# A 128-long, overlapping last chunk of keys, and a new order for the first batch and the last store, in a packed attention with a gated FFN

## The chip, the cores and the metric

The kernel runs on 1 core of one Trainium2 chip. The metric is the device time of one execution in microseconds (us). Before the change the median of 3 runs was 719.26 us, the lowest 718.98 and the highest 720.36.

## The reference

There are 8 batches, 8 heads, 576 tokens, a head width of 64, and 32 packed queries p per batch and head. Two attentions follow each other, and their output goes through a feed-forward network with a sigmoid gate:

```
P   = softmax(p k^T / 8) v            # 32 x 64 for each batch and head
x   = softmax(q P^T / 8) P            # 576 x 64 for each batch and head
h   = x @ w_in                        # x as 4608 x 512, w_in 512 x 2048
out = (h * sigmoid(1.702 h)) @ w_out  # w_out 2048 x 512
```

All of it is float32.

## The kernel before, in words

**Tiling.** The batches are worked one after the other, the first attention of batch b+1 inside the FFN of batch b. Heads go in pairs: of a pair the even head (eo = 0) lies on partitions 0 to 63 and the odd one on 64 to 127, so a 64-row product of one parity and one of the other use the two halves of TensorE's rows. The FFN is never done on x itself: `m_chunk` (L399) multiplies the small P with w_in, giving M (for each parity a tile of 128 rows: 4 heads of 32 packed queries), and `h_mm` (L561) multiplies M with the second attention's weights `a`. Large products are kept accurate by splitting each float32 operand into an upper and a lower part (`ghi`/`glo`, `mhi`/`mlo`, `ahi`/`alo`, and both halves of `wo`) and adding three products.

**FFN of a batch.** For each of 16 blocks f of 128 hidden columns: six matmuls per half of the tokens (288), tanh on ACT (L569), the gate on DVE (L551), the upper part on ACT or DVE (L116, L118), the lower part on POOL or DVE (L548), and three matmuls 128x512 per block of 128 tokens (L621) into one of four PSUM banks `acc`. 576 tokens are four blocks of 128 and a rest of 64. The rests of two batches (a pair) are gathered in the tiles `over` and make one more product of 128 tokens, `over_mm`, into bank acc0 (`acc_over` in the profile). `over_take` copies that bank to SBUF in two halves of 256 columns, and `over_store` stores each half: 2 batches x 64 rows x 256 columns. For the last pair this is the end of the program: the two copies, on ACT (L116) and DVE (L118), and the two stores (L660).

**First attention of a batch.** Scores of p with the keys (L247), in two halves of 288 keys; a maximum (L272 in batch 0), exp (`exp1`, L318; L311 in batch 0); then the weights are transposed. `turn1_mm` (L337) transposes four chunks of 128 keys per parity, `turn1_last_mm` (L348) the last 64 keys of both, and `turn1_copy` and `turn1_last_copy` copy them from PSUM to the tile `aT`. `pack` (L370) multiplies them with v: for each parity five chunks of keys, and in each chunk four products of 32 packed queries by 64 columns, which lie side by side on TensorE's columns. Each float32 product takes two passes, so a batch has 2 x 5 x 4 x 2 = 80 rows in the trace. Chunks 0 to 3 have 128 keys ("128*32" in the profile: 128 rows, 32 columns of the array), chunk 4 has 64 ("64*32"). `pack_end` (L383) divides by the sums on ACT, `pack_turn_mm` (L389) transposes P. v is loaded as two parts: `v` (512 keys) and `v_last` (64 keys, 64 partitions x 2 KB).

**Second attention.** `scores2_mm` (L451), DVE's `scores2_turn` (L462), `max2` (L482), POOL's `sub2` (L486), exp on ACT (L490), `sum2` (L495 to L497), `norm2` on POOL, and `turn2` (L507) back to key-major, whose result `xt` is split into `ahi` and `alo` for `h_mm`. For batch 0 the lower part is made on TensorE (`a_lower_mm`, L522 and L523).

**Weights.** w_in and w_out arrive as 8-byte words and are decoded: `load_w` (SP's queue), `begin_w` (ACT, L205), `join_w` (DVE, L217); `upper_w` and `lower_w` (L229) split w_out. Entries 0 to 3 of the list are the four row blocks of w_in's first 512 columns, loaded in two halves, 4 to 7 the first four blocks of w_out, and so on. `warm` (L124) issues matmuls of the identity that nobody uses.

**Order.** Nothing is scheduled by a program: the tuple `order` (L668 and on) lists every step, and each engine gets its instructions in that order; the steps take the engine as an argument (`dve`, `act`, `pool`), ACT being what most take without one. All loads and stores are issued by SP.

Of the kernel before, what the change touches and what calls it, by code (L numbers as in the profile page):

```python
# [21 lines left out]
def kernel(  # L22
# [111 lines left out]
    def load(what, b, part):  # L134
# [124 lines left out]
    def scores1_first(eo, half):  # L259

        if half == 0:
            new1(0, eo)
        if eo == 1:
            bank = ps_acc.tile([P, FC], F32, tag=f"acc{half}", name=f"ps1_0_{eo}_{half}")
        else:
            bank = bank_b(f"ps1_0_{eo}_{half}")
        for j in range(NP):
            mm1(0, eo, half, bank, j)
        st["bank", eo, half] = bank
# [60 lines left out]

    def turn1_mm(b, eo):
# [13 lines left out]
    def turn1_last_mm(b):  # L345
        st["bank", "t", b] = bank = bank_b(f"pstl_{b}")
        for e in range(2):
            nc.tensor.transpose(  # L348
                bank[:KLAST, e * P : (e + 1) * P], st["x", 1, b, e][:, (KC - 1) * P :], ident
            )  # L350

    def turn1_last_copy(b, engine=nc.scalar):
        move(
            engine,
            st["aT", b][:KLAST, KC - 1, :, :],
            st["bank", "t", b][:KLAST, : 2 * P].rearrange("p (e n) -> p e n", n=P),
        )

    def pack(b, eo=None, banks=(bank_b,)):
# [4 lines left out]
        for e in range(2) if eo is None else (eo,):  # L364
            bank = st["bank", "P", b][e if len(st["bank", "P", b]) > 1 else 0]
            for c in range(KC):
                kk = P if c < KC - 1 else KLAST
                for j in range(NP):
# [3 lines left out]
                        aT[:kk, c, e, 32 * j : 32 * j + 32],  # L372
                        vt[:kk, c, e0 : e0 + D],
# [277 lines left out]

    def over_take(pair, k, engine=nc.scalar):
        if k == 0 or pair == B // 2 - 1:
            taken["over"] = o_tile(f"o_over_{pair}_{k}")
        taken["over", pair, k] = o = taken["over"][:, columns(k)]
        move(engine, o, accs[0][:, columns(k)])

    def over_store(pair, k):
        rest = out.rearrange("(b s) d -> b s d", s=S)[2 * pair : 2 * pair + 2, S - REST :, columns(k)]
        nc.sync.dma_start(rest, taken["over", pair, k])  # L660
# [8 lines left out]
        (warm, 2, 3), (warm, 4, 2), (load, "k", 0, 0), (load, "k", 0, 1), (scores1_first, 0, 0),  # L669
        (max1_first, 0, 0), (warm, 6, 2), (scores1_first, 0, 1), (scores1_first, 1, 0),  # L670
        (max1_first, 0, 1), (load_w, 1, 0), (bias1, 0, 0), (exp1_first, 0, 0),
        (scores1_first, 1, 1), (max1_first, 1, 1), (exp1_first, 0, 1), (max1_first, 1, 0),
        (bias1, 0, 1), (sum1, 0, 0), (turn1_mm, 0, 0), (turn1_copy, 0, 0, dve), (load, "v", 0, 0),
        (exp1_first, 1, 0), (exp1_first, 1, 1), (sum1, 0, 1), (load, "v", 0, 1), (warm, 10, 3),
        (turn1_mm, 0, 1), (turn1_last_mm, 0), (turn1_last_copy, 0), (turn1_copy, 0, 1, dve),
        (load_w, 0, 0), (pack, 0, 0, late), (pack, 0, 1), (begin_w, 0, 0), (join_w, 0, 0),
        (pack_end, 0), (pack_turn_mm, 0), (load_w, 2, 0), (begin_w, 2, 0), (join_w, 2, 0),
        (load, "q", 0, 0), (pack_turn_copy, 0), (scores2_mm, 0, 0), (begin_w, 1, 0),
        (load, "q", 0, 1), (join_w, 1, 0), (warm, 7, 3), (scores2_turn, 0, 0, 0),
        (scores2_turn, 0, 0, 1), (max2, 0, 0, 0), (max2, 0, 0, 1), (load_w, 3, 0), (load_w, 3, 1),  # L680
        (begin_w, 3, 0), (sub2, 0, 0, 0, pool), (exp2, 0, 0, 0), (begin_w, 3, 1),
        (scores2_mm, 0, 1, late), (scores2_turn, 0, 1, 0), (join_w, 3, 0),
        (m_chunk, 0, 0, early, 0), (m_upper, 0, 0, 1, 0), (warm, 3, 3), (sub2, 0, 0, 1, pool),
        (scores2_turn, 0, 1, 1), (sum2, 0, 0, 0), (warm, 5, 2), (max2, 0, 1), (join_w, 3, 1),
        (norm2, 0, 0, 0, pool), (turn2, 0, 0, 0), (load_w, 0, 1), (begin_w, 0, 1), (load_w, 4),
        (exp2, 0, 0, 1), (sum2, 0, 0, 1), (warm, 8, 3), (load_w, 6), (begin_w, 4), (join_w, 4),
        (load_w, 1, 1), (sub2, 0, 1, None, pool), (norm2, 0, 0, 1, pool), (a_upper, 0, 0, 0),
        (a_lower_mm, 0, 0, 0, bank_b), (exp2, 0, 1), (sum2, 0, 1), (load_w, 2, 1),
        (turn2, 0, 0, 1), (upper_w, 4), (begin_w, 1, 1), (a_lower_copy, 0, 0, 0),
        (m_upper, 0, 0, 0, 0), (warm, 0, 3), (warm, 9, 3), (m_lower, 0, 0, 0, 0),  # L690
        (a_upper, 0, 0, 1), (a_lower_mm, 0, 0, 1, bank_b), (a_lower_copy, 0, 0, 1),
        (m_lower, 0, 0, 1, 0), (h_mm, 0, 0, 0), (join_w, 0, 1), (norm2, 0, 1, None, pool),
        (turn2, 0, 1), (lower_w, 4), (begin_w, 2, 1), (join_w, 2, 1), (h_tanh, 0, 0, 0),
        (a_upper, 0, 1, None), (a_lower, 0, 1), (h_mm, 0, 1, 0), (h_tanh, 0, 1, 0), (load_w, 5),
# [692 lines left out]
```

## Time and profile before

| what | value |
|---|---|
| median of 3 runs | 719.26 us (718.98 to 720.36) |
| the profiled execution, its own time | 720.15 us |
| its span in the trace | 718.4 us, 718.37 in the windows |
| instructions | 13002 |
| TensorE (PE) busy | 701.6 us, 98% of the span |
| mean clock granted to TensorE | 0.995 |
| moved by DMA | 55.87 MB, 78 GB/s over the span |

"PE" is the matmul side of TensorE, "PEld" its weight loads, which run beside it. In a row of a timeline stand the start in us, how long the group lasts, engine, line, operation, output and inputs, then the rows and columns of the array for PE (as in 128*32), the tile's shape, the count, and in brackets how long the engine had been idle before and what ended that. A matmul's end is modelled in the trace and runs into the next one, so distances between starts are the safer measure on PE.

### The profile page before, as it was taken

Reading aid. Unit: us, or ns where it says so; the run is one execution under the profiler, and the core shown is the slowest. Engines: PE = TensorE matmul, PEld = TensorE weight load, DVE = VectorE, ACT = ScalarE, POOL = GpSimd, SP = SyncE. Lnnn points to the kernel's source line nnn. Section 1 sums busy time; section 2 is a strip of 40 time slices with the busy share of each in tenths; the row PEclk is TensorE's granted clock in tenths of the full one; section 3 lists DMA queues with packets and bytes.
Section 4 is the critical chain, followed back from the end, with each engine's and each line's share of the span. In section 5 each row is a group of like instructions: output and inputs, shape, how many; then the busy total and the mean of one; then the engine's idle time right before and its main releaser. Section 6 shows DMA issues by size and latency. Waiting matters only on the chain.

```text
span 718.4 us, 13002 instructions
## 1 busy us (share of the span) xinstructions
PE 701.6 (98%) x5092; PEld 569.6 (79%) x5092; DVE 404.4 (56%) x1026; ACT 278.2 (39%) x672; POOL 145.7 (20%) x171
## 2 busy tenths in 40 slices
PE   7999999999999999999999999999999999999994
PEld 5767778878888888888787788877888878888883
DVE  3978885436554366335635457643775547755541
ACT  3777645423323334453322433433342433333220
POOL 1733433122501223222332123102100000000000
PEclk9999999999999999999999999999999999999998
DMA  9787503310203103121110400213210100010001
GB/s 319 311 307 253 189 0 129 96 38 1 81 17 120 39 8 131 43 88 49 60 52 3 165 0 1 96 34 119 69 49 23 66 18 1 16 44 1 1 16 58
DMA packets 17292, 55.87 MB, mean 78 GB/s; under 512 B 1872, under 2 KB 3920, under 8 KB 16208
## 3 DMA queue, kind: packets, MB, share of 16 engines
q1 hardware_dynamic: 17232, 55.05, 22.0%
q8 instruction: 40, 0.66, 0.4%
q14 instruction: 20, 0.16, 0.1%
HBM read 45.60 MB, written 9.44 MB: 77 GB/s over the span
## 4 chain that ended last, share of the span: by engine, by line
PE 93%; DVE 2%; DMA 2%; ACT 1%; issue 0%; SPq 0%; ACTq 0%
PE acc L621 48%; PE h L561 28%; PE acc_over L621 6%; PE psm_None L399 4%; PE pspv L370 2%; DMA raw<-w_in 2%; PE ps L247 1%; PE ps L451 1%; PE pst L337 1%; DMA k<-pk 1%; PE warm L124 1%; ACT top L205 0%; DVE wo L229 0%; DVE w_in L217 0%; DVE mx L482 0%
## 5 line engine op out<-in xcount | busy, mean ns | idle before, releaser
L621 PE MATMUL acc<-wo,ghi 128*128 128x512 f32 x1024 | 323.9, 397 | 1.5 <-DVE ghi L118 0.8
L621 PEld LDWEIGHTS acc<-wo,ghi 128*128 128x128 f32 x1024 | 179.3, 188 | 42.6 <-issue 14.5
L621 PE MATMUL acc<-wo,glo 128*128 128x512 f32 x512 | 201.9, 394 | 0.1
L569 ACT ACTIVATE g<-h 128x288 f32<-128x288 f32 x256 | 104.0, 411 | 242.3 <-PE h L561 226.9
L551 DVE SCALAR_TENSOR_TENSOR g<-g,h 128x288 f32<-128x288 f32 (+1 forms) x256 | 105.4, 416 | 159.0 <-ACT g L569 158.2
L548 POOL TENSOR_TENSOR glo<-g,ghi 128x224 fp32r<-128x224 f32 (+1 forms) x122 | 93.3, 775 | 307.9 <-ACT ghi L116 201.7
L561 PE MATMUL h<-ahi,mhi 128*128 128x288 f32 x512 | 145.5, 299 | 0.9 <-DVE g L551 0.6
L561 PE MATMUL h<-ahi,mlo 128*128 128x288 f32 x512 | 143.0, 295 | 0.0
L621 PEld LDWEIGHTS acc<-wo,glo 128*128 128x128 f32 x512 | 96.1, 188 | 24.0 <-DVE glo L548 0.9
L561 PEld LDWEIGHTS h<-ahi,mhi 128*128 128x128 f32 x512 | 96.2, 188 | 17.9 <-DVE x L462 5.4
L561 PE MATMUL h<-alo,mhi 128*128 128x288 f32 x512 | 108.6, 293 | 0.0
L561 PEld LDWEIGHTS h<-ahi,mlo 128*128 128x128 f32 x512 | 96.3, 188 | 7.0
L116 ACT CAST ghi<-g 128x224 fp32r<-128x224 f32 (+1 forms) x159 | 62.5, 405 | 59.5 <-DVE g L551 37.1
L561 PEld LDWEIGHTS h<-alo,mhi 128*128 128x128 f32 x512 | 82.0, 188 | 0.2 <-POOL alo L530 0.2
L548 DVE TENSOR_TENSOR glo<-g,ghi 128x224 fp32r<-128x224 f32 (+1 forms) x134 | 59.0, 450 | 17.5 <-ACT ghi L116 14.6
L551 DVE SCALAR_TENSOR_TENSOR over<-g,h 128x64 f32<-128x64 f32 x128 | 27.4, 215 | 35.1 <-ACT g L569 34.8
L427 DVE TENSOR_TENSOR mlo<-psm_None,mhi 128x512 fp32r<-128x512 f32 x62 | 42.0, 683 | 5.3 <-ACT mhi L116 4.8
L621 PE MATMUL acc_over<-wo,ghi_over 128*128 128x512 f32 x128 | 39.8, 392 | 0.0
L116 ACT CAST mhi<-psm_None 128x512 fp32r<-128x512 f32 x45 | 26.1, 586 | 30.3 <-PE psm_None L399 30.3
L118 DVE CAST ghi<-g 128x224 fp32r<-128x224 f32 (+1 forms) x97 | 31.6, 333 | 5.6 <-PE acc L621 2.4
L399 PE MATMUL psm_None<-w_in,PT 64*32 64x512 f32 x496 | 34.0, 596 | 0.0
L621 PEld LDWEIGHTS acc_over<-wo,ghi_over 128*128 128x128 f32 x128 | 23.6, 188 | 4.7
(85 smaller groups left out, 498.3 us busy)
## 6 DMA issues: line engine op xcount, KB each, us to landing
q<-q SPq DMA_DIRECT2D x16, 576.0 KB, 5.8
v<-v SPq DMA_DIRECT2D x8, 1024.0 KB, 5.3
o<-o SPq DMA_DIRECT2D x32, 256.0 KB, 2.3
raw<-w_out SPq DMA_DIRECT2D x16, 511.8 KB, 8.2
raw<-w_in SPq DMA_DIRECT2D x12, 511.8 KB, 7.5
k<-pk SPq DMA_DIRECT2D x8, 640.0 KB, 3.9
k<-pk SPq DMA_DIRECT2D x8, 576.0 KB, 5.2
raw<-w_in SPq DMA_DIRECT2D x8, 255.8 KB, 9.8
```

Source lines behind the costliest of these rows:

```text
L116: nc.scalar.copy(dst, src)
L118: engine.tensor_copy(dst, src)
L124: nc.tensor.matmul(t[:, :P], ident, ident, start=True, stop=True)
L247: nc.tensor.matmul(bank[32 * j : 32 * j + 32, :NH], kq["p", b][rows(eo), j, :], kq["k", b][rows(eo), half, j, :], start=True, stop=True,)
L370: nc.tensor.matmul(bank[32 * j : 32 * j + 32, e * D : (e + 1) * D], aT[:kk, c, e, 32 * j : 32 * j + 32], vt[:kk, c, e0 : e0 + D], start=(c ...
L399: nc.tensor.matmul(banks[eo][32 * j : 32 * j + 32, columns(part)], PT[rows(eo), j, :], w_in_sb[fc][rows(eo), j, columns(part)], start=True ...
L427: nc.vector.tensor_tensor(lo, bank[:, at], hi.bitcast(F32), op=ALU.subtract)
L548: engine.tensor_tensor(lo, src, hi.bitcast(F32), op=ALU.subtract)
L551: nc.vector.scalar_tensor_tensor(dst, th, 1.0, h, op0=ALU.add, op1=ALU.mult)
L561: nc.tensor.matmul(h[:, :NH], m[eo][part][:, fo : fo + P], a[:, eo * NH : (eo + 1) * NH], start=(n == 0), stop=(n == len(terms) - 1),)
L569: nc.scalar.activation(g, st["h", b, f, half][:, :NH], AF.Tanh, scale=1.702)
L621: nc.tensor.matmul(acc, gp[:, at : at + P], wo[f][:, part, :], start=(start and i == 0), stop=(stop and i == 2),)
```

## The change

**The last chunk of keys.** `v_last` now holds the last 128 keys (448 to 575) on 128 partitions, and `turn1_last_mm` transposes the last 128 keys of each parity. The first 64 of these are in chunk 3 already; `turn1_last_copy` multiplies them by zero: its scale is a column `mask` of 64 zeros and 64 ones, written once by two memsets on POOL. On ACT it is an activation (Copy) with that scale, in batches 1 to 7; in batch 0 it is a `tensor_scalar` on DVE. All products of `pack` now have 128 rows.

**The first scores.** In batch 0 `scores1_first` takes both parities of a half of the keys in one step, alternating between them.

**The first batch's order.** All steps of batch 0 up to block 8 (`(h_mm, 0, 8, 0)`) stand in a new order, with other engines for some and `warm` in other places; the first loads are k, k, v, v_last, then the weights, where before the first block of weights came ahead of v. From that step on the order is that of before, but for the copies of `over`.

**The over product's copy and store.** One copy of 128x512 on DVE in place of two of 128x256, for all four pairs, and two stores of 64 full rows (one per batch) in place of two of 2 x 64 x 256.

```
             else:
-                nc.sync.dma_start(t[:KLAST, main:], v_last[b])
+                nc.sync.dma_start(t[:, main:], v_last[b])
...
-    def scores1_first(eo, half):
...
+    def scores1_first(half):
+
+        for eo in range(2):
+            if half == 0:
+                new1(0, eo)
+            st["bank", eo, half] = (bank_acc(half) if eo else bank_b)(f"ps1_0_{eo}_{half}")
         for j in range(NP):
-            mm1(0, eo, half, bank, j)
-        st["bank", eo, half] = bank
+            for eo in range(2):
+                mm1(0, eo, half, st["bank", eo, half], j)
...
+    mask = cst.tile([P, 1], F32, name="mask")
+    nc.gpsimd.memset(mask[: P - KLAST], 0.0)
+    nc.gpsimd.memset(mask[P - KLAST :], 1.0)
...
-                bank[:KLAST, e * P : (e + 1) * P], st["x", 1, b, e][:, (KC - 1) * P :], ident
+                bank[:, e * P : (e + 1) * P], st["x", 1, b, e][:, S - P :], ident
...
     def turn1_last_copy(b, engine=nc.scalar):
-        move(
-            engine,
-            st["aT", b][:KLAST, KC - 1, :, :],
-            st["bank", "t", b][:KLAST, : 2 * P].rearrange("p (e n) -> p e n", n=P),
-        )
+        dst = st["aT", b][:, KC - 1, :, :]
+        src = st["bank", "t", b][:, : 2 * P].rearrange("p (e n) -> p e n", n=P)
+        if engine is nc.scalar:
+            nc.scalar.activation(dst, src, AF.Copy, scale=mask)
+        else:
+            engine.tensor_scalar(dst, src, mask, None, op0=ALU.mult)
...
-                kk = P if c < KC - 1 else KLAST
...
-                        aT[:kk, c, e, 32 * j : 32 * j + 32],
-                        vt[:kk, c, e0 : e0 + D],
+                        aT[:, c, e, 32 * j : 32 * j + 32],
+                        vt[:, c, e0 : e0 + D],
...
-    def over_take(pair, k, engine=nc.scalar):
-        if k == 0 or pair == B // 2 - 1:
-            taken["over"] = o_tile(f"o_over_{pair}_{k}")
-        taken["over", pair, k] = o = taken["over"][:, columns(k)]
-        move(engine, o, accs[0][:, columns(k)])
+    def over_take(pair, engine=nc.scalar):
+        taken["over"] = o_tile(f"o_over_{pair}")
+        move(engine, taken["over"], accs[0])
...
-        rest = out.rearrange("(b s) d -> b s d", s=S)[2 * pair : 2 * pair + 2, S - REST :, columns(k)]
-        nc.sync.dma_start(rest, taken["over", pair, k])
+        at = (2 * pair + k + 1) * S - REST
+        nc.sync.dma_start(out[at : at + REST, :], taken["over"][k * REST : (k + 1) * REST, :])
...
-        (store, 7, 1), (over_take, 3, 0), (over_take, 3, 1, dve), (over_store, 3, 1),
-        (over_store, 3, 0),
+        (store, 7, 1), (over_take, 3, dve), (over_store, 3, 1), (over_store, 3, 0),
...
-        "v_last": v[:, last:],
+        "v_last": v[:, S - P :],
```

Three places show what the order moves. The first is PE at the first scores of batch 0, before and then after; `ps_0_0`, `ps_0_1` are the banks of parity 0 and 1, the next digit the half, `pst` the transposed weights and `pstl` their last chunk.

```order
L124 MATMUL warm_111<-ident 128x128 x2
L247 MATMUL ps_0_0_1_114<-k_100 32x288 x4
L247 MATMUL ps_0_1_0_121<-k_100 32x288 x4
L247 MATMUL ps_0_1_1_133<-k_100 32x288 x4
L337 MATMUL pst_0_148<-ident,x_0_0_103 128x128 x4
L124 MATMUL warm_164<-ident 128x128 x3
L337 MATMUL pst_1_168<-ident,x_0_1_119 128x128 x4
L348 MATMUL pstl_173<-ident,x_0_0_103 64x128
```

```order
L247 MATMUL ps_0_0_1_125<-k_104 32x288
L247 MATMUL ps_0_1_1_126<-k_104 32x288
L124 MATMUL warm_138<-ident 128x128 x3
L340 MATMUL pst_0_146<-ident,x_0_0_107 128x128 x4
L124 MATMUL warm_153<-ident 128x128 x3
L340 MATMUL pst_1_166<-ident,x_0_1_110 128x128 x4
L351 MATMUL pstl_172<-ident,x_0_0_107 128x128
```

The two parities of a half now alternate, the `warm` matmuls that stood between the halves stand behind the scores, and the last chunk's transpose has 128 rows.

The second is DVE between batch 0's second scores and the first `xt`, which the first `h_mm` needs, before and then after.

```order
L482 TENSOR_REDUCE mx_0_0_257<-x_0_0_237 128x9 x2
L462 STREAM_TRANSPOSE x_0_1_267<-ps_0_1_0_268 128x288
L217 SCALAR_TENSOR_TENSOR w_in_79<-raw_260,top_86 128x256
L462 STREAM_TRANSPOSE x_0_1_267<-ps_0_1_1_269 128x288
L495 TENSOR_REDUCE sm_0_0_299<-x_0_0_237 128x9
L496 TENSOR_SCALAR sm_0_0_299<-sm_0_0_299 128x9
L497 RECIPROCAL rs_0_0_300<-sm_0_0_299 128x9
L482 TENSOR_REDUCE mx_0_1_307<-x_0_1_267 128x18
L217 SCALAR_TENSOR_TENSOR w_in_79<-raw_260,top_83 128x256
L507 STREAM_TRANSPOSE xt_0_311<-x_0_0_237 128x288
```

```order
L485 TENSOR_REDUCE mx_0_0_259<-x_0_0_247 128x9
L217 SCALAR_TENSOR_TENSOR w_in_79<-raw_243,top_83 128x256
L217 SCALAR_TENSOR_TENSOR w_in_79<-raw_243,top_86 128x256
L498 TENSOR_REDUCE sm_0_0_285<-x_0_0_247 128x9
L499 TENSOR_SCALAR sm_0_0_285<-sm_0_0_285 128x9
L500 RECIPROCAL rs_0_0_286<-sm_0_0_285 128x9
L465 STREAM_TRANSPOSE x_0_1_291<-ps_0_1_0_292 128x288
L465 STREAM_TRANSPOSE x_0_1_291<-ps_0_1_1_293 128x288
L485 TENSOR_REDUCE mx_0_1_307<-x_0_1_291 128x18
L118 CAST mhi_0_0_312<-psm_0_0_0_273 128x256
L510 STREAM_TRANSPOSE xt_0_316<-x_0_0_247 128x288
```

Both weight decodes now come ahead of the sums, the second half's two turns behind them, and a copy of M (`mhi`) has come to DVE from ACT, ahead of `xt`.

The third is SP's queue at the end of the program, before and then after; `o_over` is the copy of the last over product, the four others are blocks of the last batch.

```order
L641 DMA o<-o_2_7711 128x512
L641 DMA o<-o_3_7731 128x512
L641 DMA o<-o_0_7703 128x512
L641 DMA o<-o_1_7705 128x512
L660 DMA o<-o_over_1_7778 2x64x256
L660 DMA o<-o_over_0_7776 2x64x256
```

```order
L644 DMA o<-o_2_7711 128x512
L644 DMA o<-o_3_7731 128x512
L644 DMA o<-o_0_7703 128x512
L644 DMA o<-o_1_7705 128x512
L660 DMA o<-o_over_7776 64x512 x2
```

The stores stand where they stood; only the shape of the last two is another.

More of the change, by code (lines that the diff above doesn't have):

```diff
@@ L668 @@
     order = (
[L669 to L692, printed above, removed]
@@ L735 @@
[L735 to L739 removed]
+        (warm, 8, 3), (warm, 2, 3), (load, "k", 0, 0), (load, "k", 0, 1), (scores1_first, 0),
@@ new lines @@
+        (pack, 0, 1), (pack_end, 0), (pack_turn_mm, 0), (load_w, 0, 0), (pack_turn_copy, 0, dve),
+        (begin_w, 1, 0), (load, "q", 0, 0), (begin_w, 0, 0), (join_w, 0, 0), (load_w, 3, 0),
+        (load_w, 3, 1), (join_w, 1, 0), (scores2_mm, 0, 0), (scores2_turn, 0, 0, 0),
+        (max2, 0, 0, 0), (scores2_turn, 0, 0, 1), (max2, 0, 0, 1), (warm, 4, 2), (begin_w, 3, 1),
+        (join_w, 3, 1), (warm, 6, 2), (begin_w, 3, 0), (join_w, 3, 0), (m_chunk, 0, 0, early, 0),
+        (sub2, 0, 0, 0, pool), (exp2, 0, 0, 0), (sum2, 0, 0, 0), (load, "q", 0, 1),
@@ L1230 @@
+        (out_mm, 6, 5, 2), (h_gate, 6, 7, 1), (out_mm, 6, 6, 2), (h_mm, 6, 8, 0),
         (h_tanh, 6, 8, 0), (h_gate, 6, 8, 0), (out_mm, 6, 5, 1), (out_mm, 6, 6, 1),
```

269 lines of the change are left out of this document (139 added, 130 removed).

## The prediction

> **What bounds the kernel now.** I read the page's busy shares and its chain first, to see whose time the program is, and then the windows by stage, to see where that engine is not working.
>
> ```profile
> PE 701.6 (98%) x5092; PEld 569.6 (79%) x5092; DVE 404.4 (56%) x1026; ACT 278.2 (39%) x672; POOL 145.7 (20%) x171
> PE 93%; DVE 2%; DMA 2%; ACT 1%; issue 0%; SPq 0%; ACTq 0%
> 0.00:4.70 4.70, 2.50 (x10) 2.21 (x10) 0.00 (x0) 1.69 (x3) 2.56 (x10) 1.00 0.58 203
> 4.70:9.70 5.00, 4.44 (x36) 1.74 (x36) 1.55 (x5) 0.60 (x3) 0.00 (x0) 1.00 0.98 345
> 9.70:26.60 16.90, 14.95 (x185) 10.93 (x186) 12.61 (x38) 9.96 (x27) 5.45 (x6) 1.00 1.03 386
> 26.60:65.00 38.40, 36.91 (x254) 27.92 (x253) 31.22 (x70) 28.72 (x62) 18.48 (x17) 1.00 0.84 296
> 65.00:708.74 643.74, 642.75 (x4610) 526.81 (x4608) 358.63 (x917) 236.86 (x577) 119.24 (x139) 1.00 0.16 54
> 708.74:718.37 9.63, 0.00 (x1) 0.00 (x0) 0.42 (x1) 0.37 (x1) 0.00 (x0) 0.65 0.09 27
> ```
>
> The windows give the stretch, its length, each engine's busy time (PE, PEld, DVE, ACT, POOL), the granted clock, the DMA share and GB/s. PE works 642.75 of the 643.74 us from the step at which the two orders meet again (65.00) to the last product: there only PE's own work counts. Time without PE lies at the two ends: 9.63 us after the last product, 1.49 (38.40 less 36.91) and 1.95 (16.90 less 14.95) in batch 0, where the DMA share is 0.84 to 1.03. So three sums: the tail, the packs of batches 1 to 7, and the start.
>
> **The tail.** The timeline of the last microseconds, and the DMA view of 709 to 719 us (40 slices of 0.25 us).
>
> ```profile
> 708.34 0.40 PE L621 MATMUL acc_over<-wo,glo_over 128*128 128x512 f32 x1
> 708.82 0.37 ACT L116 COPY o_over<-acc_over 128x256 f32<-128x256 f32 x1 [14.63 <-PE acc_over L621]
> 709.23 0.42 DVE L118 COPY o_over<-acc_over 128x256 f32<-128x256 f32 x1 [6.91 <-ACT o_over L116]
> 709.68 1.14 SPq L660 DMA_DIRECT2D o<-o_over  x2
> GB/s 0 0 0 0 0 0 0 25 16 41 49 16 49 33 12 45 49 49 49 49 45 49 49 45 49 49 49 49 49 45 49 37 0 0 0 0 0 0 0 0
> q1 hardware_dynamic: 260, 0.26, 8.2%
> ```
>
> The two copies stand one after the other, although they are on two engines. The stores issue from 709.68 on, move from 710.75 to 717.0 at 49 GB/s at most, and 1.4 us later the span ends (718.37). The change is priced by a store of the same 256 KB in the middle of the program, its issue and its DMA view (626 to 628 us, slices of 0.05), and by the group of whole-bank copies on DVE.
>
> ```profile
> 626.08 0.33 SPq L641 DMA_DIRECT2D o<-o  x1
> GB/s 0 0 0 0 0 0 0 0 0 0 0 0 0 0 0 0 0 0 287 246 369 492 287 492 369 328 492 287 492 287 410 246 123 41 0 0 0 0 0 0
> L118 DVE COPY o<-acc 128x512 f32<-128x512 f32 x16 | 10.9, 685 | 5.6 <-PE acc L621 5.6
> ```
>
> That store's packets begin 0.82 us after its issue (626.90) and last 0.8 us, at up to 492 GB/s, ten times the last store's. The new stores have 64 rows in the slowest place of both patterns, as this one has 128, and rows of the same 2 KB; the old ones have 2 batches there. New tail: the DVE copy starts at 708.82 where ACT's did and takes 0.685, to 709.51; issue at 709.54 (0.03 later, as before); the second one half of 1.14 behind, 710.11; packets 0.82 later, 710.93, for half of 0.8, 711.33; and 1.4 to the end: 712.7. The tail is 4.0 us in place of 9.63: **5.6 us less**. Bounds: 4.8 if issue and first packet are as late as in the old tail (709.68 to 710.75 is 1.07, and the issues do not overlap), 5.9 if the second issue takes the 0.33 of the single store.
>
> The Trainium skill, "DMA: Bandwidth & Descriptors", section "Why a DMA increments its semaphore by 16 and not by 1", has a transfer use as many of 16 engines as divide the slowest dimension: two for the old stores, 16 for the new. The trace agrees, by 49 against 492 GB/s. The same page's rules for kernel authors advise one transfer of 128 partitions over two of half as many, which speaks against the new pair: going by the single store above, one transfer would end at 709.54 + 1.62 + 1.4 = 712.56, and the sum would be 0.17 better. But the rows of the two batches do not lie together in the output, so it is no choice here.
>
> **The packs.** PE in batch 1's pack: whole, and then at three narrow windows, where a change of form splits the groups; then ACT's copy of the last chunk, and in batch 6 the load that waits for one.
>
> ```profile
> 73.42 0.38 PE L348 MATMUL pstl<-ident,x 128*64 128x128 f32 x2
> 73.73 1.73 PE L370 MATMUL pspv<-v,aT 128*32 128x64 f32 x80
> 75.39 0.40 PE L561 MATMUL h<-ahi,mhi 128*128 128x288 f32 x1
> 73.95 0.44 PE L370 MATMUL pspv<-v,aT 128*32 128x64 f32 x16
> 74.32 0.32 PE L370 MATMUL pspv<-v,aT 64*32 64x64 f32 x8
> 74.56 0.26 PE L370 MATMUL pspv<-v,aT 128*32 128x64 f32 x4
> 73.84 0.37 ACT L116 COPY aT<-pstl 64x256 f32<-64x256 f32 x1
> 488.18 0.35 ACT L116 COPY aT<-pstl 64x256 f32<-64x256 f32 x1
> 488.58 0.15 PEld L370 LDWEIGHTS pspv<-v,aT 64*32 64x32 f32 x8 [0.17 <-ACT aT L116]
> ```
>
> One matmul of the pack lasts 0.22, so the last of the sixteen from 73.95 starts at 74.17 (0.44 less 0.22, starts 0.056 apart for each four), and the 64-row form begins 0.15 later, not 0.036 (0.056 less the 0.020 that four take). The eight end their starts at 74.42, and the next form begins 0.14 later; its first four then need 0.08 in place of 0.056. One change thus costs 0.11 + 0.024 = 0.135 us. It happens three times inside a pack (128 to 64 rows, back, and again to 64); entry and exit keep theirs. Removed: 0.405 us a batch; a check is 20 fours x 0.056 + 0.405 + 0.135 for the two that stay = 1.66, which is 75.39 less 73.73.
>
> What is late next is the masked copy: chunk 4's weights need it, and it comes sooner now. Unforced, chunk 4 would start at 73.73 + 0.08 + 7 x 0.056 = 74.21. The transposes end at 73.80, the copy starts 0.04 later, and the load follows its end by 0.05 (488.53 to 488.58). Its length with a scale taken from a tile is in no row; nearest are exponentials that differ by a bias from a tile:
>
> ```profile
> L318 ACT ACTIVATE x<-x,nb 128x576 f32<-128x576 f32 x14 | 10.9, 777 | 3.4 <-DVE nb L302 3.3
> L490 ACT ACTIVATE x<-x 128x576 f32<-128x576 f32 x15 | 10.3, 685 | 14.6 <-DVE x L486 14.3 <-POOL x L486 0.3
> ```
>
> 92 ns more, so 0.37 + 0.09 = 0.46, and chunk 4 starts at 74.35: a wait of 0.14. Left are 0.26 a batch. In batch 6 the load waits for the copy already, which covers one change, and the longer copy is paid in full: 0.405 - 0.135 - 0.09 = 0.18. Six times 0.26 and 0.18 are **1.7 us** over batches 1 to 7. Bounds: 2.4 with a copy at the old 0.37, 1.3 with 0.50, 2.8 without a wait. Behind the longer copy on ACT's queue stand 0.09 us of delay for a weight cast or a tanh, covered by ACT's 39%. v_last's second 128 KB per batch costs nothing where the DMA share is 0.16. The over copies of pairs 0 to 2 move to DVE (56%) at 0.685; bank acc0 is freed 0.1 us sooner than by two serial copies of 0.37 and 0.42: nothing.
>
> **The start.** PE's and ACT's rows in batch 0 on which the term rests.
>
> ```profile
> 4.77 1.18 PE L247 MATMUL ps<-k 64*32 64x288 f32 x8 [0.91 <-DMA k<-pk]
> 7.04 2.17 PE L247 MATMUL ps<-k 64*32 64x288 f32 x24
> 37.97 0.71 PE L247 MATMUL ps<-k 64*32 64x288 f32 x16
> 10.70 1.49 PE L124 MATMUL warm<-ident 128*128 128x128 f32 x6
> 20.77 2.05 PE L124 MATMUL warm<-ident 128*128 128x128 f32 x16
> 17.05 0.72 PE L451 MATMUL ps<-q,PT 64*32 64x288 f32 x16 [0.35 <-ACT PT L116]
> 25.88 0.75 PE L522 MATMUL psal<-xt,ident 128*128 128x288 f32 x2 [0.53 <-DVE xt L507]
> 26.60 0.30 PE L561 MATMUL h<-ahi,mhi 128*128 128x288 f32 x1
> 50.74 0.50 PE L621 MATMUL acc<-wo,ghi 128*128 128x512 f32 x1 [0.71 <-POOL wo L229]
> 51.37 2.03 ACT L205 CAST top<-raw 128x512 f16<-128x512 bf16 x3 [2.41 <-DMA raw<-w_in]
> 53.74 0.73 PE L621 MATMUL acc<-wo,ghi 128*128 128x512 f32 x2 [0.78 <-DVE ghi L118]
> 65.01 0.30 PE L561 MATMUL h<-ahi,mhi 128*128 128x288 f32 x1
> ```
>
> Sixteen alternating score passes took 0.71 in batch 1; the same warm matmuls take 0.25 each at 10.70 and 0.13 at 20.77, so PE's early pace is half, and two times 16 take some 2.6 us from 4.77: the scores are done near 7.4, not 9.2, if the keys' second half is there. Following exp, transposes and the pack through the new order with these durations, I get about 0.9 us of lead at the second scores (16.1 for 17.05). It is lost again on DVE: the second half's two turns and maximum and a copy of M now stand ahead of the first `xt` (the order's second place), some 1.5 us, and a decode ahead of the second. The first `h_mm` comes near 26.7, level with 26.60, by 0.5 either way. From there to 65.01 PE has the same products; its idle time of 1.49 us is just the two named waits, 0.71 for the lower part of w_out and 0.78 for `ghi`, and the latter stands behind ACT's 2.41 us for a landing of w_in. In the new order the splits of w_out and of `g` stand further ahead of their products, and no load of w_in is needed earlier. I take nearly all of it: **1.4 us**. Bounds: 2.5 with the lead kept too; 2.4 us lost if one weight lands as late as that at ACT's place, with PE behind it. v_last's second 128 KB, at 386 GB/s, is 0.34 us of delay for the weights behind it, inside these bounds.
>
> The sum: 5.6 + 1.7 + 1.4 = 8.7 us. From the profiled execution's 720.15 (its 718.37 and 1.78 around it) that is 711.45; that execution was 0.89 above the median, so on the median 719.26 - 8.7 = 710.6.
>
> **The rivals.** *The start gives nothing.* DVE and POOL as busy as before (31.22 and 18.48 of 38.40 us) make new waits where the old ones went: 712.0, and down to a loss of 2.4, 714.4. For it: the lead was lost once already by 26.6. *The wait takes the packs' gain.* The masked copy lasts 0.7 and ends all of the 0.405: 712.3. Against it: no ACT row of that size is as long. *The tail is latency, not bandwidth.* The end waits for something like 1.4 us after each of two stores in turn, or the packets begin late: a gain of 3 us, 713.2. Against it: the 6.2 us of packets at 49 GB/s. *Slower.* ACT's in-order queue: in batch 0 each `begin_w` waits for its landing, with casts and tanh of the FFN behind it, and PE behind those. If the new order puts waits like the 2.41 us one on PE's path three to five times, the start loses 9 us and the time is 719.26 - 7.3 + 9 = 721; it decides from a loss of 7.3 on. Against it: one such wait in 38 us before, of which PE saw 0.78. The Trainium skill, "TensorE: Matmul & The Clock Gate", Part 1 on the clock gate, says that an idle window of about 3.4 us halves TensorE's clock; PE standing that long would then run at the early half pace for a while, which would bring the deciding loss at fewer waits; the granted clock here is 1.00 in every window to 708.74. *The change doesn't do what it says*, if a form change were paid by the row groups and not the form: then packs are as now, 712.3 again.
>
> **How the numbers follow.** The forecast's own case, all three terms within their bounds, has 0.64, the start without gain 0.18, packs without gain 0.07, the short-changed tail 0.06, slower 0.03, and 0.02 for losses that add up to within 0.2% (1.4 us, about what a measurement can tell). The best of all bounds is 719.26 - 5.9 - 2.4 - 2.5 = 708.5, the worst of the forecast with the start's loss 719.26 - 4.8 - 1.3 + 2.4 = 715.6. The range leaves out the last 1.2 of that: 708.4 to 714.4. Faster 0.95, same 0.02, slower 0.03.
>
> **What would show it.** Right: about 4 us from the last product to the end, with the last packets on 16 engines; about 1.4 us for a pack's 80 rows, and a load of chunk 4 that waits 0.1 to 0.2 for ACT's copy of 0.46; `h_mm` of block 8 near 63.6. Wrong: a tail over 5 us, a pack of 1.66 still, or that step later than 65.

## The result, and the profile after

The changed kernel takes 712.99 us (median of 4 runs, 712.67 to 713.31), the kernel before 719.51 beside it (718.98 to 720.36). The ratio is 0.9908 (0.9891 to 0.9925): 6.5 us less, where 8.7 was forecast. The range holds it. The profiled executions are 6.9 us apart in span (718.4 and 711.5), and the parts below are taken from these two.

First the page's engine line of the changed kernel, then its windows, cut at the same three places as before: the first product with w_in, block 8 of batch 0, and the end of the last product.

```profile
PE 698.0 (98%) x5092; PEld 567.8 (80%) x5092; DVE 404.6 (57%) x1027; ACT 277.3 (39%) x668; POOL 144.7 (20%) x172
```

```profile
0.00:25.27 25.27, 18.80 (x232) 13.02 (x233) 13.87 (x42) 12.13 (x31) 7.74 (x18) 1.00 0.94 362
25.27:61.25 35.98, 35.71 (x255) 27.53 (x254) 30.71 (x69) 28.91 (x65) 18.90 (x17) 1.00 0.78 299
61.25:706.75 645.50, 643.48 (x4610) 527.28 (x4608) 359.33 (x917) 236.24 (x574) 118.02 (x138) 1.00 0.17 57
706.75:711.49 4.74, 0.00 (x0) 0.00 (x0) 0.69 (x1) 0.00 (x0) 0.00 (x0) 0.78 0.25 55
```

Block 8 is reached at 61.25 in place of 65.01, 3.8 us earlier, with 0.27 us without PE in the second window in place of 1.49. The tail is 4.74 in place of 9.63, 4.9 less. But the long middle is longer: 645.50 in place of 643.74, although the packs in it are shorter by 1.5. So some 3.2 us were lost in a stretch in which the forecast had allowed for no loss. The sum is 3.8 + 4.9 - 1.8 = 6.9.

The tail, by the timeline and the DMA view of 707 to 712 us (40 slices of 0.125 us, and the queue's share of the time of 16 engines):

```profile
706.35 0.40 PE L624 MATMUL acc_over<-wo,glo_over 128*128 128x512 f32 x1
706.84 0.69 DVE L118 COPY o_over<-acc_over 128x512 f32<-128x512 f32 x1 [6.58 <-PE acc_over L624]
707.55 1.11 SPq L660 DMA_DIRECT2D o<-o_over  x2
```

```profile
GB/s 0 0 0 0 0 0 0 0 0 0 0 0 0 131 262 131 246 197 197 246 147 229 229 66 17 0 0 0 0 0 0 0 0 0 0 0 0 0 0 0
q1 hardware_dynamic: 160, 0.26, 23.9%
```

Packets now move for 1.5 us (708.63 to 710.13) where they moved for 6.2. By the slices they begin 1.08 us after the first issue, and the end comes 1.4 us after the last.

The pack of batch 1: the whole of it on PE, and ACT's masked copy.

```profile
69.98 1.51 PE L373 MATMUL pspv<-v,aT 128*32 128x64 f32 x80
71.42 0.40 PE L564 MATMUL h<-ahi,mhi 128*128 128x288 f32 x1
```

```profile
70.08 0.47 ACT L359 ACTIVATE aT<-pstl,mask 128x256 f32<-128x256 f32 x1
```

From first product to the next work it is 1.44 (71.42 less 69.98) in place of 1.66, in five others the same, and 1.58 in place of 1.74 in batch 6. That is 6 x 0.22 + 0.15 = 1.46 us.

The start on PE, with the waits for DVE: from the first scores' end to the first product with w_in.

```profile
7.44 1.65 PE L124 MATMUL warm<-ident 128*128 128x128 f32 x6
9.05 0.96 PE L340 MATMUL pst<-ident,x 128*128 128x128 f32 x4
9.84 0.83 PE L124 MATMUL warm<-ident 128*128 128x128 f32 x6
11.33 1.60 PE L373 MATMUL pspv<-v,aT 128*32 128x64 f32 x80
14.75 0.72 PE L454 MATMUL ps<-q,PT 64*32 64x288 f32 x16 [0.39 <-DVE PT L118]
18.12 0.41 PE L402 MATMUL psm<-w_in,PT 64*32 64x256 f32 x2 [0.99 <-DVE w_in L217]
21.67 0.75 PE L525 MATMUL psal<-xt,ident 128*128 128x288 f32 x2 [1.13 <-DVE xt L510]
25.27 0.30 PE L564 MATMUL h<-ahi,mhi 128*128 128x288 f32 x1
```

In the kernel before the first transposes start at

```profile
9.74 1.17 PE L337 MATMUL pst<-ident,x 128*128 128x128 f32 x4 [0.53 <-ACT x L311]
```

The lead is 0.7 us at these transposes, 2.1 at the pack (13.40 before), 2.3 at the second scores and 1.3 at the first product. Here six `warm` matmuls take 1.65 us at 7.44 and 0.83 at 9.84; in the kernel before such matmuls still take 0.25 each at 10.70.

And one of the places where the middle lost time, batch 4 at 374 us: the over copy of pair 1, a gate behind it on DVE, and the next batch's first scores on PE.

```profile
374.10 0.67 PE L247 MATMUL ps<-k 64*32 64x288 f32 x2
374.21 0.69 DVE L118 COPY o_over<-acc_over 128x512 f32<-128x512 f32 x1 [2.59 <-PE acc_over L624]
374.82 0.45 DVE L554 SCALAR_TENSOR_TENSOR g<-g,h 128x288 f32<-128x288 f32 x1
375.32 0.47 PE L247 MATMUL ps<-k 64*32 64x288 f32 x7 [0.55 <-DVE g L554]
```

The scores begin at 374.10 and get stuck until the gate ends, since they go into the bank that it reads. In the kernel before the sixteen ran through.

### The profile page after: what moved, and what is told of

It is laid out like the page before. It is cut to its first block, busy times and chain, and to the rows that moved or that the text cites. A ratio compares the mean times of both kernels' runs of the same rounds, so it can differ in the third digit from the quotient of the medians.

```text
span 711.5 us, 12984 instructions
## 1 busy us (share of the span) xinstructions
PE 698.0 (98%) x5092; PEld 567.8 (80%) x5092; DVE 404.6 (57%) x1027; ACT 277.3 (39%) x668; POOL 144.7 (20%) x172
## 4 chain that ended last, share of the span: by engine, by line
PE 93%; DVE 4%; ACT 1%; DMA 1%; issue 0%; SPq 0%; DVEq 0%; ACTq 0%
PE acc L624 49%; PE h L564 28%; PE acc_over L624 6%; PE psm_None L402 4%; PE ps L247 1%; PE ps L454 1%; PE pspv L373 1%; PE pst L340 1%; DMA k<-pk 1%; DVE w_in L217 1%; DVE x L465 0%; DVE wo L229 0%; PE warm L124 0%; ACT top L205 0%; DVE mx L485 0%
## 5 line engine op out<-in xcount | busy, mean ns | idle before, releaser
L551 POOL TENSOR_TENSOR glo<-g,ghi 128x288 fp32r<-128x288 f32 (+1 forms) x119 | 89.7, 764 | 310.6 <-ACT ghi L116 195.0
L116 ACT CAST ghi<-g 128x288 fp32r<-128x288 f32 (+1 forms) x161 | 63.3, 406 | 60.8 <-DVE g L554 39.7
L551 DVE TENSOR_TENSOR glo<-g,ghi 128x288 fp32r<-128x288 f32 (+1 forms) x137 | 60.4, 451 | 19.2 <-ACT ghi L116 15.9
```

The costliest lines, as they stand in the source:

```text
L116: nc.scalar.copy(dst, src)
L551: engine.tensor_tensor(lo, src, hi.bitcast(F32), op=ALU.subtract)
```

## The experiments

Twelve kernels, each with its ratio to the kernel before. The profiled executions were compared matmul by matmul as well, pairing each with its counterpart.

**1. The tail alone** (in the kernel before, for the last pair only):

```
+        if pair == B // 2 - 1:
+            taken["over"] = o_tile(f"o_over_{pair}")
+            move(engine, taken["over"], accs[0])
...
+            nc.sync.dma_start(out[at : at + REST, :], taken["over"][k * REST : (k + 1) * REST, :])
```

> The kernel before with one part of the change alone: only the last pair's over product gets the single 128x512 copy on DVE and the two stores of 64 full rows. Theory A, the parts add: the stretch from the last product to the end goes from 9.63 to about 4.7 us, as in the changed kernel, everything ahead of it stays, and the time is 4.9 us lower (719.5 to 714.6, ratio 0.993). Rival B, part of the shorter tail only appears with the other parts: less than 4 us lower.

714.32 us, ratio 0.9930 (0.9918 to 0.9943): 4.9 us less. The last product ends at 708.24, the span at 713.05, a tail of 4.8. Theory A; the tail adds to the rest as it is.

**2. The last chunk alone** (its diff is that of the change):

> The kernel before with the 128-long last chunk alone (v_last, transposes, masked copy, products), in all batches; order, first scores, over copies and stores are those of before. Theory A: each pack of batches 1 to 7 goes from 1.66 (1.74 in batch 6) to 1.44 (1.58), the load of chunk 4 waiting 0.15 for a copy of 0.47; 1.5 us lower in all, ratio 0.998. Rival B: the longer copy on ACT and the second 128 KB of v_last delay something behind them, and the time stays within 0.5 us of before.

717.30 us, ratio 0.9968 (0.9956 to 0.9979), 2.0 less (1.5 to 3.2 by the interval). From batch 2's pack to the last product, with six of the packs, the trace has 553.55 us in place of 554.53: the six give 1.25, and 0.2 is lost again at 488. Rival B falls. But the execution was also 2.6 us ahead at batch 1's pack, with an order in batch 0 that is that of before. The waits of PE for the weights' and `g`'s upper parts tell why, in this kernel's, experiment 1's, experiment 7's and the kernel before's execution, which all have the order of before in batch 0: none in this one, and in the others, from their start to 74 us,

```profile
PE acc L621 <- DVE ghi L118: 0.8, 1, 0.8
PE acc L621 <- POOL wo L229: 0.7, 1, 0.7
```

in the kernel before,

```profile
PE acc L621 <- POOL wo L229: 0.3, 1, 0.3
PE acc L621 <- DVE ghi L118: 0.3, 1, 0.3
```

in experiment 1, and in experiment 7 one of 0.9. Experiment 1 has a third one besides, at 56.7 us:

```profile
PE h L561 <- ACT x L116: 0.4, 1, 0.4
```

From the first product with w_in to block 8 the same 252 matmuls take 38.4 us in the kernel before, 38.2 in experiment 1, 37.3 in experiment 7 and 36.3 in this one, and 35.9 to 36.0 in all nine kernels with the whole new order up to block 8. So the waits on which the forecast's third term rests change from one execution to the next. The profiled one, 0.89 above its median, had both in full.

**3. The start alone** (in the kernel before: the new order up to block 8, and the new first scores):

> The kernel before with the first batch's new order and first scores alone (the last chunk stays 64 long). Block 8's first product of batch 0 was at 65.01 before and is at 61.25 in the changed kernel. Theory A: it comes at about 61.3 here too, and the whole 3.7 us reach the end, since what the changed kernel lost between block 8 and its last product has another cause (the over copy on DVE, and an execution's slightly longer pitch of PE): ratio 0.995. Rival B: the early lead is taken back by later waits that the order brings (loads that come too late for a batch that is ahead), and less than 2.5 us reach the end.

718.36 us, ratio 0.9990 (0.9981 to 0.9999): 0.9 less. Block 8 did come at the changed kernel's time: batch 1's pack starts at 69.98, as there. Of the 3.75 us of lead there 1.34 reached the end of the span. So theory A fails in its second half. Two things took 2.4 us. One is what B put: a landing that comes too late. A weight decode on ACT (`begin_w`) waits 2.06 us for a load of w_out, and with it come late the two decodes and the copy of batch 1's last chunk behind it:

```profile
65.45 0.78 ACT L205 CAST top<-raw 128x512 f16<-128x512 bf16 x1 [2.06 <-DMA raw<-w_out]
69.74 1.41 ACT L205 CAST top<-raw 128x512 f16<-128x512 bf16 x2
71.00 0.37 ACT L116 COPY aT<-pstl 64x256 f32<-64x256 f32 x1
71.42 0.51 PE L368 MATMUL pspv<-v,aT 64*32 64x64 f32 x12 [0.79 <-ACT aT L116]
```

It cost PE 0.85 us. The other eight kernels with the whole new order have this wait too, of 0.3 to 1.2 us, and there PE loses 0.07 at most; why the landing was later here is not shown. The other thing is nearly all no wait: from batch 2's pack to the last product the work takes 555.88 us in place of 554.53, spread over thousands of matmuls.

**4. The over copies of pairs 0 to 2 in halves** (in the changed kernel):

```
-(over_take, 1, dve), (h_gate, 4, 2, 0), (scores1_mm, 5, 0, inner), ...
+(over_take, 1, 0), (h_gate, 4, 2, 0), (over_take, 1, 1, dve), (scores1_mm, 5, 0, inner), ...
```

> The changed kernel, but the over copies of pairs 0 to 2 again as two halves of 256 columns on the engines of before (the last pair's copy and all stores as changed). Theory A: in the changed kernel the copy of pair 1 (0.69 us on DVE at 374.21) stands ahead of a gate whose bank the next batch's first scores need, and PE waits 0.9 to 1.2 us longer there; with the halves that wait is gone and the time is about 1 us lower than the changed kernel's (ratio to the kernel before 0.9895 instead of 0.991). Rival B: that wait comes from the batch being 3.5 us earlier than before (a load or the gate's own input is late), and stays.

711.97 us, ratio 0.9896 (0.9881 to 0.9912), 1.0 below the changed kernel's median. The intervals of the two ratios overlap, so the place decides: in the trace the changed kernel loses 1.2 us at this one place against the kernel before, and this one nothing. Theory A. The gate now stands ahead of DVE's half of the copy; the first half is ACT's.

**5. The gate ahead of the copy** (in the changed kernel):

```
-(over_mm, 1, 3), (over_take, 1, dve), (h_gate, 4, 2, 0),
+(over_mm, 1, 3), (h_gate, 4, 2, 0), (over_take, 1, dve),
```

> The changed kernel with two neighbours swapped in the order: the gate of batch 4, block 2, ahead of pair 1's over copy on DVE instead of behind it. Theory A, PE's wait at 374 us was for the gate, which stood behind a copy of 0.69 us: the swap alone takes 0.9 to 1.2 us off, as the halves did (713.0 to about 712.0). Rival B, the whole-bank copy itself holds something up (bank acc0): the wait moves to the next product into acc0, and less than 0.5 us is gained.

712.31 us, ratio 0.9910 (0.9896 to 0.9923): the time alone does not tell it from the changed kernel. The place does. PE and DVE at 374 us:

```profile
374.28 0.72 PE L247 MATMUL ps<-k 64*32 64x288 f32 x16
374.39 0.69 DVE L118 COPY o_over<-acc_over 128x512 f32<-128x512 f32 x1 [1.32 <-PE acc_over L624]
374.79 1.06 PE L402 MATMUL psm_None<-w_in,PT 64*32 64x512 f32 x16
```

The sixteen scores run through, and the 1.2 us that the changed kernel loses here are not lost; bank acc0 holds nothing up. Theory A: the profiled span is 1.2 us shorter (710.3 for 711.5), though this execution came 0.4 later to block 8, and the median 0.7 lower. The wait was the gate's place in DVE's queue, and the longer copy mattered only by standing ahead of it.

**6. Old places for the buffers.** All tiles of the working pool get their place in SBUF in the order in which the program first asks for them. So the new order of batch 0 also moved most of the buffers: by the sizes in the two lists of places, `ghi` lies 4096 bytes higher, `wo5` 23936 lower, and so on. This kernel is experiment 4's with the places of before:

```
+    layout = (
+        ("kqv", 2560, 2), ("x", 576, 5), ("mx1", 2, 2), ("wo13", 1024, 1), ...
+    )
+    for tag, n, bufs in layout:
+        for i in range(bufs):
+            wk.tile([P, n], F32, tag=tag, name=f"first_{tag}_{i}", bufs=bufs)
```

> The kernel with the over copies in halves (the changed kernel, pairs 0 to 2 copied as before), with one thing more: every buffer in SBUF is given its place before any work, in the order in which the kernel before first uses them. No instruction changes but its addresses, which are again those of before plus 32 bytes (the mask). From block 8 on, kernels with the new first order lose 1.6 to 2 us to 706 us in matmuls that each start a few ns later, and the kernels with the old order lose nothing. Theory A, it is the place of the operands in SBUF, which follows the order of first use: with the old places the loss goes, and the time is 1.5 to 2 us lower than with the halves alone (712.0 to about 710.3, ratio to before 0.9874). Rival B, it is something else that the new order leaves behind (which of a rotating set of buffers or banks a tile gets, or the engines' phase): nothing changes, 712.

710.96 us, ratio 0.9879 (0.9864 to 0.9895), 1.0 below experiment 4 where 1.5 to 2 were expected; from batch 2's pack to the last product 553.93 us in place of 554.69. The intervals of the two ratios overlap, so here too the pairing decides: of 475 distances between a `ghi` and the `glo` matmul that follows, behind 85 us, this kernel has 260 to the nanosecond as in the kernel before (experiment 1, with the old order, 341; experiment 3 only 93, experiment 4 81). Theory A in kind, with about half of the size.

**7. New places for the buffers** (the kernel before, with experiment 3's places):

> The kernel before, with its order and everything else untouched, but its SBUF buffers placed beforehand as the kernel with the new first order has them. Theory A: its matmuls after block 8 get slower by 1.5 to 2 us in all, 719.4 to about 721.1, ratio 1.0024. Rival B: as before, ratio 1.000.

720.32 us, ratio 1.0011 (1.0000 to 1.0021): 1.1 more. The start of batch 2's pack and the last product, in the kernel before

```profile
153.81 0.30 PE L370 MATMUL pspv<-v,aT 128*32 128x64 f32 x6
...
708.34 0.40 PE L621 MATMUL acc_over<-wo,glo_over 128*128 128x512 f32 x1
```

and in this one

```profile
153.02 0.37 PE L386 MATMUL pspv<-v,aT 128*32 128x64 f32 x12
...
708.68 0.40 PE L637 MATMUL acc_over<-wo,glo_over 128*128 128x512 f32 x1
```

554.53 us there and 555.66 here, by the same instructions in the same order, so that experiment 6's rival B falls too. Theory A, with 1.1 us where 1.5 to 2 were expected; the interval of the times alone reaches down to no change. Summed over all paired distances behind 85 us (those that differ by less than 60 ns), the kernels with the old places stand at -0.27 to +0.21 us against the kernel before (experiments 1, 2, 6 and 12) and those with the new places at +0.67 to +1.45 (the changed kernel and all the others; experiment 8's places are nearly the new ones). Without the packs, which experiments 10 and 12 shorten, it is +0.10 to +0.27 and +1.01 to +1.47. Two chips ran the experiments, and both groups hold runs of both. Which buffers' places do it, and by what way, is open.

**8. New order to the first product, then the old one** (in the kernel before):

> The kernel before (64-long last chunk, old over copies and stores) with the new first scores and the new order up to batch 0's first product with w_in (26.60 before, 25.27 in the changed kernel), and from there the steps that are left in the order of before. It tells the two parts of the start's 3.76 us apart: 1.33 ahead of the first product and 2.43 after it. Theory A, they add: the first product comes at about 25.3, the two waits of before (0.9 us each by the starts, for the split of w_out and for ghi) stay, and block 8 comes at about 63.7. Rival B, PE only arrives sooner at weights that land no earlier: the waits grow by the lead and block 8 is back at 65.

718.75 us, ratio 1.0000 (0.9988 to 1.0013). The first product comes at 24.65, 1.95 ahead. The lead is not eaten: batch 1's pack is at 70.73, 3.0 ahead. Of the two waits one was there, and longer:

```profile
48.96 0.49 PE L619 MATMUL acc<-wo,ghi 128*128 128x512 f32 x1 [1.14 <-POOL wo L229]
```

Theory A in that the lead stays; but block 8 comes at 61.97 and not at 63.7, since the first product was 0.65 earlier than expected and the other wait was absent, as it is in some executions of the old order. By the times nothing is left of the lead: the new places cost 1.4 us on the way to the end, and the kernel before does not have both waits in every execution. The rest is not accounted for.

**9. The old stores behind the one copy** (in the changed kernel):

```
-        nc.sync.dma_start(out[at : at + REST, :], taken["over"][k * REST : (k + 1) * REST, :])
+        rest = out.rearrange("(b s) d -> b s d", s=S)[2 * pair : 2 * pair + 2, S - REST :, columns(k)]
+        nc.sync.dma_start(rest, taken["over"][:, columns(k)])
```

> The changed kernel with its one copy of the over product, but stored as before in two stores of 2 x 64 rows x 256 columns. Theory A, the stores' form is nearly all of the shorter tail: last product to end about 9.5 us (9.63 before, less 0.14 for one copy instead of two), the time 4.75 us above the changed kernel's, 717.7, ratio to before 0.9975. Rival B, the copies were worth a good part, the second store waiting for the second copy: 7 to 8 us of tail.

717.92 us, ratio 0.9982 (0.9972 to 0.9992). The issue and the DMA view of 706 to 716 us (slices of 0.25):

```profile
706.74 1.08 SPq L660 DMA_DIRECT2D o<-o_over  x2
```

```profile
GB/s 0 0 0 0 0 0 0 16 16 37 45 16 41 37 20 37 49 49 49 49 49 45 45 49 49 49 49 49 49 49 49 45 8 0 0 0 0 0 0 0
```

At most 49 GB/s again, and a tail of 9.56. Theory A: the form of the stores is nearly all of it, the single copy 0.1.

**10. The masked copy in two** (in the changed kernel):

```
-            nc.scalar.activation(dst, src, AF.Copy, scale=mask)
+            for e in range(2):
+                nc.scalar.activation(dst[:, e, :], src[:, e, :], AF.Copy, scale=mask)
```

> The changed kernel, but the masked copy of the last chunk as two activations on ACT, one for each parity (128x128 instead of 128x256; batch 0's copy on DVE is as it was). Theory A, chunk 4 of parity 0 waits only for its own half: about 0.36 us instead of 0.47, so the load's wait of 0.15 nearly goes, packs go from 1.44 to about 1.30 and the time by 0.9 us (713.0 to 712.1). Rival B, the products wait for both activations, which last longer together: packs of 1.7, the time 1.7 us higher.

712.62 us, ratio 0.9912 (0.9899 to 0.9926): not told from the changed kernel by the time. Each pack did get shorter, by 0.11 us to 1.34:

```profile
69.98 1.41 PE L374 MATMUL pspv<-v,aT 128*32 128x64 f32 x80
71.32 0.40 PE L565 MATMUL h<-ahi,mhi 128*128 128x288 f32 x1
```

So the wait for the copy is real, theory A by the place; in the sum 0.4 us of the expected 0.9 show, for 0.26 us were lost again right behind the pack of batch 1, and as much in batch 6, where PE waits for a lower part that does not come sooner:

```profile
74.94 0.49 PE L625 MATMUL acc<-wo,glo 128*128 128x512 f32 x1 [0.61 <-DVE glo L552]
```

**11. The last store issued by ACT** (in the changed kernel):

```
+        queue_ = nc.scalar if pair == B // 2 - 1 and k == 0 else nc.sync
+        queue_.dma_start(out[at : at + REST, :], taken["over"][k * REST : (k + 1) * REST, :])
```

> The changed kernel, but the very last store is issued by ACT instead of SP, so that the two last stores are issued at the same time. Theory A, the second issue on SP is half a microsecond late and its packets with it: the tail goes from 4.74 to about 4.2 us. Rival B, the tail is set by a fixed latency between an issue and its first packets and between the last packet and the end, or issuing from ACT is slower: no change within 0.2 us.

712.32 us, ratio 0.9910 (0.9896 to 0.9923). The two issues now lie side by side:

```profile
707.71 0.47 SPq L661 DMA_DIRECT2D o<-o_over  x1
707.71 0.56 ACTq L661 DMA_DIRECT2D o<-o_over  x1
```

The tail by the trace is 4.43 (706.90 to 711.33), 0.3 less than the changed kernel's: theory A, smaller than thought. The time alone does not tell it, but the tail hardly varies: 4.77 to 4.81 by the trace in the six kernels with the new stores on SP alone (4.77 in the changed kernel, cut at 4.74 above), and 4.43 here and in experiment 12.

**12. All repairs in one** (experiments 4, 6, 10 and 11 together):

> All repairs in one: the changed kernel with the over copies of pairs 0 to 2 in halves as before, the buffers of SBUF placed as before, the masked copy in two activations, and the last store issued by ACT. If the parts add: 1.0 (over copies) + 1.0 (places, measured) + 0.9 + 0.5 = 3.4 us below the changed kernel, about 709.6, ratio to before 0.986. If the earlier time is taken up by waits for weights in batch 0 and 1: 710.5 or more.

709.92 us, ratio 0.9877 (0.9864 to 0.9891): 3.1 below the changed kernel's median (2.2 by the two ratios, 3.3 by the two spans), and the fastest of all. Of the expected 3.4 us 2.2 to 3.3 came: the parts add for the most part. The windows of its last two stretches, for comparison with those of the changed kernel:

```profile
60.86:703.74 642.88, 641.06 (x4610) 526.66 (x4608) 358.49 (x916) 238.87 (x585) 118.24 (x138) 1.00 0.17 57
703.74:708.17 4.43, 0.00 (x1) 0.00 (x0) 0.69 (x1) 0.00 (x0) 0.00 (x0) 0.92 0.22 59
```

The middle, from block 8 at 60.86 on, is 642.88 in place of 645.50, 0.9 below the kernel before. Its packs are shorter by 2.2 in all, so more than half of that is still lost, 1.1 of it at the two places of experiment 10.

## Why the prediction was right, and where not

**The tail** was right in its mechanism (experiments 1 and 9) and 0.7 too large: 4.9 for 5.6. Two terms of the sum were too small. The first packet was taken to come 0.82 us after the issue, as behind a store in the middle of the program. It came after 1.08, which is just what the old tail's rows had shown (709.68 to 710.75), and the bound of 4.8 came from them. And the packets were to move for 0.97 us (710.36 to 711.33), by half of the single store's 0.8 for each store; they moved for 1.5, at 262 GB/s at most where the single store had 492. By the queue's share, the old stores' packets took 13.1 us of engine time (8.2% of 16 engines for 10 us) in 6.2 us, which is 2.1 engines at a time, and the new ones' 19.1 us (23.9% for 5 us) in 1.5, which is 12.7. By this estimate it is the number of engines, and not the shorter rows of the old stores (1 KB for 2 KB), that held them at 49 GB/s. The trace bears out the Trainium skill's "DMA: Bandwidth & Descriptors", section "Why a DMA increments its semaphore by 16 and not by 1": same copy, same bytes, 49 GB/s with a slowest dimension of 2 and up to 262 with one of 64.

**The packs** were right: 0.22 a batch for 0.26, 1.46 for 1.7, with a copy of 0.47 for the estimated 0.46. The wait for it is real (experiment 10): by the starts chunk 4 begins 0.16 us late, for an estimated 0.14.

**The start** had the wrong size, 3.8 for 1.4, and came the wrong way there. The first step that failed is PE's early pace. The forecast carried the half pace of before through transposes and pack ("with these durations") and got a lead of 0.9 us at the second scores; it was 2.3. The alternating scores were done at 7.5, as forecast, and gave 0.7 at the first transposes. But these, six `warm` matmuls and the last transposes took 2.28 us up to the pack, where they had taken 3.66 (9.74 to 13.40): `warm` matmuls start 0.213 us apart at 10.7 to 11.6 in the kernel before, and 0.112 apart at 9.8 to 10.3 here. The trace's record of the granted clock begins, with 1.00, at 15.36 there and at 9.65 here; the windows show 1.00 ahead of it as well, where there is no record. It begins at 14.1 to 15.6 in the four executions with the old start, and with the new one at 9.7 to 10.9 in six and at 4.3 to 5.9 in four, whose first product comes at 24.7 to 25.0 in place of 25.3 to 25.8. Why the new start gets the full pace so much sooner is not shown.

"It is lost again on DVE" was right for 1.0 us only (the waits at 18.12 and 21.67), so the first product came 1.3 ahead, not level. The two waits behind it went, as forecast: nine profiled executions with the whole new order up to block 8 have none. They were worth more than their 1.49, since a matmul's modelled end covers part of a wait; by the starts they were 0.88 and 0.95. With the lead of 1.33 that is 3.2 of the 3.8; the rest is spread over the stretch, which takes 36.3 us with the old order even without the two waits (experiment 2) and 36.0 here. But the waits were partly the profiled execution's own bad luck: block 8 comes at 62.4 to 65.0 in the four executions with the old order and at 60.6 to 61.7 in the nine, which is 2.8 us on the average. The forecast, which took its size from one execution, had no row that could have shown that.

**The middle** is where the forecast broke. "There only PE's own work counts", and the over copies "nothing", were two steps:

- The price of the over copies looked at bank acc0, which the copy frees, and not at what is queued behind the copy on DVE. For pair 1 that was a gate that the next scores wait for: 1.2 us in the trace (experiments 4 and 5).
- That the products after block 8 are the same instructions was taken to mean the same time. Their operands had moved, and that cost 0.8 to 1.4 us (experiments 3, 6 and 7; 1.45 in the changed kernel by the paired distances).

Some 0.3 us went at 74.77 in batch 1 and 0.2 at 488 in batch 6, where PE now arrives ahead of a lower part. By the profiles, 3.76 + 4.89 + 1.46 less 1.21, 1.45 and 0.53 is 6.92, and 6.88 were measured. That the sum came within 2.2 us of the forecast's is in part luck: the start gave 2.4 us more than was forecast, the middle lost 3.2 that were not, and the tail fell 0.7 short.

Of the rivals none came true by itself. "The start gives nothing" named the right loss, new waits on DVE, at the wrong place. The landing that ACT waits for, of "Slower", is in the trace of all nine kernels with the new order, once in each, and cost PE 0.85 us in experiment 3 alone. "1.00 in every window" held where the clock is on record, from 9.65 us to the last product in the changed kernel; in experiment 12's execution 0.50 was granted from 14.56 to 17.98 us.

## What to carry to other kernels

Price a longer instruction not only by what it frees but by what stands behind it on its engine: a copy of 0.69 us ahead of a gate, on an engine that is 57% busy, cost 1.2 us of PE. Where places in SBUF follow the order of first use, an edit at the start of a program also moves the buffers of all later work; compare the distances of unchanged matmuls before looking for a wait, and fix the places if they matter. And a stage that waits for landings should be priced from several executions: with the same order the stretch that holds the two waits took 38.4, 38.2, 37.3 and 36.3 us.

## What the runs showed of the hardware

- The place of buffers in SBUF changes the distance of matmuls by a few ns each, without any wait in the profile: 0.2% of a stretch of 555 us (experiment 7).
- TensorE starts at half pace (the same 128x128 float32 matmuls 0.213 us apart, later 0.112). The record of the granted clock of 1.00, which goes with the full pace, begins at 14.1 to 15.6 us in four executions with the old start and at 4.3 to 10.9 in ten with the new one.
- A change between products of 128 and of 64 rows costs PE 0.11 us and 0.024 for the products behind it (starts 0.150 and 0.060 us apart in place of 0.036, kernel before). Taking three of them (0.405) out of a pack, at the price of a wait for the masked copy, gave 0.22.
- A store's first packets came 1.08 us after its issue at the end of the program and 0.82 for the one store read in its middle; the end of the span came about 1.4 us behind the last packet before and after the change.
